# Seven block products for the hidden-dimension transform of 1024 rows, with kept sums of the sequence matrices

## The chip, the cores and the metric

The kernel runs on one core of a Trainium2 chip. The metric is device time in microseconds (us) of one execution, median of the runs. TensorE (PE) multiplies matrices, VectorE (DVE) and ScalarE (ACT) work elementwise, GpSimd (POOL) and SyncE (SP) here mostly issue transfers (DMAs) between the core's memory (SBUF) and the device memory.

## The reference

Four layers act on x of 2048 rows and 512 columns, each as x + f(layernorm(x)). Layers 0 and 2 mix (a Fourier transform as real matrix products), layers 1 and 3 are a gated feed-forward network.

```python
def mix(x, Cs, Ss, Cd, Sd):        # Cs, Ss: 2048x2048; Cd, Sd: 512x512
    a = x @ Cd.T                   # along the hidden dimension
    b = x @ Sd.T
    return Cs @ a - Ss @ b         # along the sequence
def ffn(x, w_gate, w_up, w_down):  # 512x1792, 512x1792, 1792x512
    return (gelu(x @ w_gate) * (x @ w_up)) @ w_down
x = x + mix(layernorm(x)); x = x + ffn(layernorm(x))
x = x + mix(layernorm(x)); x = x + ffn(layernorm(x))
```

Everything is float32. The kernel's matmuls read a rounded format (fp32r); each operand is split into a high and a low part and a product is made of three matmuls, hi·hi, hi·lo and lo·hi (`mm3`, lines 194 to 198). This triple is the unit of work.

## The kernel before

`mix` exchanges the order of the two transforms: it first multiplies the normalized rows z with the sequence matrices and then the result with the hidden matrices wh (cosine, and the sine with its sign turned by `split_minus`). The 2048 output rows are four blocks b of 512 (`NB`, `TB`). Per block the sequence products are done by seven block products instead of eight, in stages `a11`, `a12`, `s2` and `s4`; a `plan` gives the order. The block pieces A11, A12, A21, A22 of the sequence matrix are streamed from device memory in 128x512 tiles, and `make_s2` and `make_s4` form the sums S1 to S4 on VectorE (S1 = A21 + A22, S3 = A11 - A21, S2 = S1 - A11, S4 = A12 - S2). Layer 0 and layer 2 use the same matrices and form the same sums, each for itself. `plain` splits a tile into its two parts: the high one by ScalarE, the low one by VectorE (`split`, lines 145 to 149).

A block's sequence products leave eight tiles `cs[m, c]` (m: cosine or sine, c: which 128 of the 512 hidden columns), each 128 columns by 512 rows. `hid_groups` then multiplies them with wh: eight slices of wh, each with the four row tiles of the block, 32 triples, added up in four banks; `x_add` adds x, row tile by row tile, and stores the new x. So the two blocks that the change joins take 64 triples. In the plan the groups stand between the stages of a block (`EARLY_HID`, `MID_HID`, `LATE_HID`).

The next layer's norms are small pieces of work (`block_steps`): `norm` loads rows of x with `x_load_mixed`, normalizes and turns them by 32x32 transposes into a `wide` tile, which is stored, and `fetch` reads it back with the hidden dimension on the partitions. They are dealt out as `chores` in `hid_groups`, or queued and run one at each `step`.

Loads and stores: SyncE issues nearly all loads, in one order; `take`, `split_next` and `load_next` keep `AHEAD` + `RAW` items of the stream ahead of the product that uses them. GpSimd issues most stores and some loads, also in one order. SBUF is 94 slots of 128x512 (`NSLOT`) handed out in turn, oldest free one first, and two wide tiles that can be lent as four more slots each. A load into a slot waits until the slot's last reader is done. A scheduler sets the order of the instructions of each engine when the program is built.

The gated layers do the gate and up products, and some of the down products (`SEVEN`), as seven block products already. Their pieces are made once in layer 1 by `weight_steps` (load, four sums, splits, stores to device memory) and loaded again later. Down products made this way come out turned: `turned_rows` transposes them by 32x32 blocks into `xturned`, a wide tile with x, and `rows_done` stores it. In layer 3 with w = 1 the stored tile (`begun`) is read back by `begun_load`, and `plain_rows` adds the last products and writes `out`: these are the last instructions of the kernel.

Of the kernel before, what the change touches and what calls it, by code (L numbers as in the profile page):

```python
# [24 lines left out]
GELU_C = 0.044715  # L25
AHEAD = 7
# [9 lines left out]
SEVEN = {(1, 1): 5, (3, 0): 7, (3, 1): 5}  # L36
FORE = {0: 4, 2: 4}
# [6 lines left out]
def fnet_geglu(ctx: ExitStack, tc: tile.TileContext, x_in, ws, wh, wgu, wdn, wdc, out):  # L44
# [182 lines left out]
    def x_load_mixed(layer, i):  # L227

        g, n = divmod(i, NT)
        t = sb.get()  # L230
        for j in range(NT):
            r0 = j * P + n * 32
            nc.sync.dma_start(t[j * 32:(j + 1) * 32], xs[layer, g][r0:r0 + 32])
        return t

    def x_add(layer, i, t, ps, keep=False, engine=nc.gpsimd):

        plus(t, t, ps)
        ps8.put(ps)
        engine.dma_start(rows(layer + 1, i), t)  # L240
        if keep:
            fresh[i] = t
        else:
            sb.put(t)

# [19 lines left out]
    def down_piece(k, name):  # L265

        i = next(i for i, names in enumerate(pieces) if name in names)
        if i == 3:
            return wdd[k][:, 3 * 1024:]
        h = half[pieces[i].index(name)]  # L270
        return wdd[k][:, i * 1024:(i + 1) * 1024].rearrange("p (h c) -> p h c", h=2)[:, :, h]
# [55 lines left out]
    s1s, s2s, s3s, cs, held = {}, {}, {}, {}, {}  # L327
# [21 lines left out]
    def make_s2(k):  # L349
        def run(a21, a22, *a11):  # L350
            a11 = a11[0] if a11 else held.pop(k)
            plus(a22, a21, a22)
            minus(a21, a11, a21)
            minus(a11, a22, a11)
            s1s[k], s2s[k], s3s[k] = a22, a11, a21
            return split_slot(a11)
        return run
# [7 lines left out]
    def make_s4(k):  # L365
# [31 lines left out]

    def plan(layer):
# [31 lines left out]
    def mix_items(layer):  # L430
# [3 lines left out]
        for b, what in plan(layer):  # L434
# [9 lines left out]
            elif what == "S2":  # L444
                for i, k in skewed(3):
                    if i == 0:
                        raw(make_s2(k), a21[k], a22[k], *(() if hold else (a11[k],)))
                    else:
                        raw(make_s1(k) if i == 1 else make_s3(k))
            elif what == "S4":  # L450
                for i, k in skewed(2):
                    if i == 0:
                        raw(make_s4(k), a12[k])
                    else:
                        raw(plain, a22[k])
            else:
# [6 lines left out]
    for layer in range(0, 4, 2):  # L463
        mix_items(layer)
        for w in range(NB // 2):
# [7 lines left out]
            else:  # L473
                for near, products in zip(NEAR[1:], down_order(layer + 1, w)):
                    items.extend((F32R, (down_piece(k, name),), whole, near) for name, k in products)
# [126 lines left out]
    def block_steps(layer, w):  # L602
# [82 lines left out]
    def mix(layer):  # L685
        hid, sums, chores, hid_left = {}, {}, [], [0]

        def chores_at(b):
            if b == NB - 3:
# [127 lines left out]
        def s4(b):  # L817
            last = b == NB - 1
            if b == NB - 4:
                sb.reclaim("z")  # L820
            one, three = sides.pop(b)
# [16 lines left out]

        stages = {"A11": a11, "A12": a12, "S2": s2, "S4": s4}
        for n, (b, what) in enumerate(plan(layer)):  # L840
# [7 lines left out]
            if what in stages:  # L848
                stages[what](b)
            else:  # L850
# [55 lines left out]
    down_making = {}  # L906
# [27 lines left out]
    def geglu(w, layer):  # L934
# [71 lines left out]
        def up(n):  # L1006
            if layer == 1 and w == 1:
# [4 lines left out]
                if n % 2 == 0 and n // 2 + 1 in down_making:  # L1012
                    queue.extend(down_making.pop(n // 2 + 1)[1])
            if n + 3 in making:
# [97 lines left out]
        def ended(name, ps):  # L1112
# [3 lines left out]
            elif name == "A22":  # L1116
                for c in range(2):
                    turned_rows(0, 2 + c, ps[c])
                    ps8.put(ps[c])
                rows_done(0)  # L1120
            else:
# [6 lines left out]
                for c in range(2):  # L1128
                    turned_rows(name != "A12", 2 * (name in ("S1", "S3")) + c, to[c])
# [26 lines left out]
        def turned_view(at, part):  # L1156

            t = begun[part] if at == layer + 1 and pairs < NP else xs[at, w * 2 + part]
            return t.rearrange("(j t) (p e) -> p t j e", t=32, e=P)

        def rows_moved(at, part, run):

            for p in range(NT):
                v = xturned[part][p * 32:(p + 1) * 32]
                run(v.rearrange("t (j e) -> t j e", e=P), turned_view(at, part)[p])

        def load_turned(part):
            assert part or not sb.out("x")
            pool = tpool if part else upool
            xturned[part] = pool.tile([P, NT * D], F32, name="wide" if part else "xwide")  # L1170
            rows_moved(layer, part, lambda v, outside: nc.sync.dma_start(v, outside))

        def turned_rows(part, c, src):

            t = sb.get()
            blocks_of = "p (j e) -> p j e"
            nc.vector.transpose(t.rearrange(blocks_of, e=32), src.rearrange(blocks_of, e=32))
            to = xturned[part].rearrange("p (j c e) -> p j c e", c=NT, e=32)[:, :, c]
            plus(to, to, t.rearrange(blocks_of, e=32))
            sb.put(t)  # L1180

        def rows_done(part):
            rows_moved(layer + 1, part, lambda v, outside: nc.gpsimd.dma_start(outside, v))  # L1183
# [218 lines left out]
```

## Time and profile before

| what | value |
|---|---|
| three runs, median (lowest to highest) | 1620.7 us (1620.21 to 1622.89) |
| profiled execution | 1620.15 us |
| span of its trace | 1618.1 us |
| mean granted TensorE clock | 0.999 |
| matmuls on record | 7066 |
| bytes moved | 424.14 MB, 262 GB/s on average |

In the profile a busy share is an average over stages. A line such as `L197 PE MATMUL p<-s,s` is one line of the code, with output and inputs by the program's names without their numbers: `s` is a slot, `p` a bank, `wc` and `wb` pieces of weights in device memory, `x` the rows. Matmuls overlap: one lasts 389 ns on record while they start much closer together, so counts and starts say more than durations.

### The profile page before, as it was taken

What the parts mean: (1) busy time and instruction counts of PE and PEld (TensorE: products, weight loads), DVE (VectorE), ACT (ScalarE), POOL (GpSimd) and SP (SyncE); (2) the same over time, 40 slices, a digit from 0 to 9 for tenths busy, and PEclk for the clock granted to TensorE, in tenths of its full rate; (3) what the DMA queues carried; (4) which work ended last, traced back from release to release, by engine and by line L of the source; (5) the groups of instructions that cost most, each with busy time, mean ns of one, the idle gap of its engine ahead of it and who ended that gap; (6) DMA issues with size and microseconds to landing.
All of it is one profiled execution on the core that took longest, in us unless ns stands there. A gap on an engine that the chain in (4) does not pass through costs nothing.

```text
span 1618.1 us, 22784 instructions
## 1 busy us (share of the span) xinstructions
PE 1608.9 (99%) x7066; PEld 1326.0 (82%) x7066; DVE 1168.5 (72%) x2041; ACT 815.8 (50%) x1557; POOL 270.5 (17%) x477
## 2 busy tenths in 40 slices
PE   9999999999999999999999999999999999999998
PEld 6888888888888888888888888888888888888886
DVE  8996877889877655667887878787864557844573
ACT  7743453645766434556565434544445535433360
POOL 3111010152544113220120000010410000000002
PEclk9999999999999999999999999999999999999999
DMA  9767787899978799887887676868989776896455
GB/s 357 256 227 256 258 274 247 272 310 321 348 274 299 228 361 335 312 303 259 260 265 242 210 259 210 309 217 298 275 279 281 231 222 198 276 289 199 138 176 156
DMA packets 244937, 424.14 MB, mean 262 GB/s; under 512 B 28816, under 2 KB 82832, under 8 KB 243792
## 3 DMA queue, kind: packets, MB, share of 16 engines
q1 hardware_dynamic: 218016, 332.75, 64.1%
q0 software_dynamic: 26800, 89.94, 15.6%
q8 instruction: 56, 0.92, 0.2%
q14 instruction: 65, 0.53, 0.1%
HBM read 336.86 MB, written 85.72 MB: 261 GB/s over the span
## 4 chain that ended last, share of the span: by engine, by line
PE 96%; DMA 2%; DVE 1%; SPq 0%; issue 0%; ACT 0%; POOL 0%; DVEq 0%
PE p L196 32%; PE p L197 32%; PE p L198 32%; DMA s<-ws 1%; DMA out<-s 1%; PE p L749 0%; DMA s<-wb 0%; DVE s L149 0%; DMA s<-begun 0%; DVE s L180 0%; DMA xwide<-t 0%; DVE s L184 0%; DVE st L506 0%; SPq L224 0%; SPq L294 0%
## 5 line engine op out<-in xcount | busy, mean ns | idle before, releaser
L197 PE MATMUL p<-s,s 128*128 128x512 f32 x2334 | 906.6, 389 | 0.0
L198 PE MATMUL p<-s,s 128*128 128x512 f32 x2334 | 894.8, 389 | 0.3 <-DMA s<-wb 0.3
L196 PE MATMUL p<-s,s 128*128 128x512 f32 x2334 | 868.0, 390 | 0.5 <-ACT s L147 0.5
L147 ACT ACTIVATE s<-s 128x512 fp32r<-128x512 f32 (+1 forms) x764 | 437.9, 608 | 335.4 <-PE p L198 61.7
L149 DVE TENSOR_TENSOR s<-s,s 128x512 fp32r<-128x512 f32 (+1 forms) x764 | 483.8, 665 | 82.1 <-ACT s L147 67.0
L196 PEld LDWEIGHTS p<-s,s 128*128 128x128 f32 x2334 | 438.1, 188 | 93.1 <-ACT s L147 1.1
L197 PEld LDWEIGHTS p<-s,s 128*128 128x128 f32 x2334 | 438.2, 188 | 92.1 <-DVE s L149 0.7
L198 PEld LDWEIGHTS p<-s,s 128*128 128x128 f32 x2334 | 438.2, 188 | 92.1 <-DMA s<-wb 0.8
L184 DVE TENSOR_TENSOR s<-s,p 128x512 f32<-128x512 f32 x295 | 198.7, 683 | 232.3 <-PE p L198 127.3
L191 ACT ACTIVATE s<-p 128x512 f32<-128x512 f32 x217 | 127.2, 592 | 124.4 <-PE p L198 119.1
L180 DVE TENSOR_TENSOR s<-s,s 128x512 f32<-128x512 f32 (+1 forms) x305 | 184.7, 622 | 3.2 <-DMA s<-t 2.0
L931 ACT ACTIVATE s<-s 128x512 f32<-128x512 f32 x103 | 64.6, 629 | 83.0 <-DVE s L184 82.5
L147 ACT ACTIVATE s<-xwide 128x512 fp32r<-128x512 f32 (+1 forms) x90 | 53.3, 604 | 74.5 <-PE p L197 20.7
L519 POOL TENSOR_SCALAR rstd<-rstd 128x1 f32<-128x1 f32 x40 | 20.7, 517 | 350.0 <-ACT s L518 316.8
L149 DVE TENSOR_TENSOR s<-xwide,s 128x512 fp32r<-128x512 f32 (+1 forms) x90 | 58.5, 660 | 22.7 <-ACT s L147 22.3
L278 POOL DMA_DIRECT2D wb<-s x84 | 45.6, 545 | 58.3 <-ACT s L147 46.0
L516 ACT ACTIVATE s<-s 128x512 f32<-128x512 f32 x33 | 20.8, 630 | 68.0 <-PE p L198 27.6
L945 DVE TENSOR_TENSOR s<-s,s 128x512 f32<-128x512 f32 x75 | 51.8, 690 | 1.8
L240 POOL DMA_DIRECT2D x<-s x40 | 22.0, 550 | 162.2 <-DVE s L184 154.9
L538 ACT ACTIVATE s<-s,shift,rstd 128x512 f32<-128x512 f32 x53 | 42.5, 810 | 10.5 <-DVE shift L511 9.1
L187 DVE TENSOR_TENSOR s<-s,s 128x512 f32<-128x512 f32 (+1 forms) x69 | 40.9, 612 | 2.6 <-DMA s<-ws 2.6
L1183 POOL DMA_DIRECT2D begun<-xwide x8 | 5.2, 656 | 218.9 <-DVE xwide L187 218.9
(98 smaller groups left out, 581.9 us busy)
## 6 DMA issues: line engine op xcount, KB each, us to landing
s<-ws SPq DMA_DIRECT2D x381, 256.0 KB, 4.4
s<-wb SPq DMA_DIRECT2D x294, 256.0 KB, 4.9
s<-wc SPq DMA_DIRECT2D x119, 256.0 KB, 4.1
s<-wh SPq DMA_DIRECT2D x116, 256.0 KB, 5.3
wb<-s POOLq DMA_DIRECT2D x98, 256.0 KB, 4.5
s<-x SPq DMA_DIRECT2D x64, 256.0 KB, 5.1
xwide<-ws SPq DMA_DIRECT2D x51, 256.0 KB, 5.2
wc<-s POOLq DMA_DIRECT2D x49, 256.0 KB, 5.4
```

Source lines behind the costliest of these rows:

```text
L147: newest["ACT"] = nc.scalar.activation(hi, src, AF.Copy)
L149: newest["DVE"] = nc.vector.tensor_tensor(lo, src, f32(hi), op=ALU.subtract)
L180: nc.vector.tensor_tensor(out, a, b, op=ALU.subtract)
L184: bank_read["DVE"] = nc.vector.tensor_tensor(out, a, b, op=ALU.add)
L191: bank_read["ACT"] = nc.scalar.activation(v, src, AF.Copy)
L196: nc.tensor.matmul(ps, ah, bh, start=start, stop=False, skip_group_check=True)
L197: nc.tensor.matmul(ps, ah, bl, start=False, stop=False, skip_group_check=True)
L198: nc.tensor.matmul(ps, al, bh, start=False, stop=stop, skip_group_check=True)
L278: nc.gpsimd.dma_start(a, f32(t))
L538: nc.scalar.activation(z, x, AF.Identity, bias=shift, scale=rstd)
L931: nc.scalar.activation(t, g, AF.Gelu_apprx_tanh)
L945: nc.vector.tensor_tensor(t, t, v, op=ALU.mult)
```

## The change

In layer 2 blocks 0 and 1 are done together (`PAIRED`). Their hidden products become one stage `H` behind both blocks' sequence products: 1024 rows times wh as seven block products over four slices and two column halves. The pieces of wh (`whp`) are made in layer 1, w = 0, from a rearranged copy `whc`, by the same `weight_steps`. The results come out turned and are added to turned x. The norms of layer 3 that stood as chores in blocks 1 and 2 are queued behind `H`. The sums S1, S2 and S3 of blocks 0 to 2 are stored by GpSimd in layer 0 (`KEPT`) and loaded in layer 2 in place of A21, A22 and A11. Three things move besides: all `fetch` transfers go to GpSimd, the loads of `x_load_mixed` are ordered behind the stream's last load, and the last `begun` store goes to SyncE.

```diff
+HID_MADE = 3, 6, 8, 10
+HID_EARLY = 9
+KEPT = [("S1", "S2", "S3")] * 3 + [()]
+PAIRED = {0: 0, 2: 1}
...
@@ x_load_mixed
-            nc.sync.dma_start(t[j * 32:(j + 1) * 32], xs[layer, g][r0:r0 + 32])
+            with tc.issue_after(stream["last"].ins):
+                nc.sync.dma_start(t[j * 32:(j + 1) * 32], xs[layer, g][r0:r0 + 32])
...
+    def turned_moves(t, outside, run):
+        view = outside.rearrange("(j t) (p e) -> p t j e", t=32, e=P)
+        for p in range(NT):
+            run(t[p * 32:(p + 1) * 32].rearrange("t (j e) -> t j e", e=P), view[p])
...
+    def turned_add(x, c, src):
+        t = sb.get()
+        blocks_of = "p (j e) -> p j e"
+        nc.vector.transpose(t.rearrange(blocks_of, e=32), src.rearrange(blocks_of, e=32))
+        to = x.rearrange("p (j c e) -> p j c e", c=NT, e=32)[:, :, c]
+        plus(to, to, t.rearrange(blocks_of, e=32))
+        sb.put(t)
...
+    whp = {c: dram.tile([P, 7 * 512], F32, name=f"wp{c}") for c in range(ND)}
...
@@ make_s2, and new makers beside it
             s1s[k], s2s[k], s3s[k] = a22, a11, a21
+            for name, v in (("S1", a22), ("S3", a21)):
+                keep_sum(b, name, k, v)
...
+    def keep_sum(b, name, k, v):
+        if (b, name, k) in keep_s and (b, name, k) not in kept_s:
+            kept_s.add((b, name, k))
+            nc.gpsimd.dma_start(keep_s[b, name, k], v)
...
+    def make_s2_kept(k):
+        def run(v):
+            s2s[k] = v
+            return split_slot(v)
+        return run
...
@@ make_s4
             v = s2s.pop(k)
+            keep_sum(b, "S2", k, v)
             minus(a12, a12, v)
...
@@ plan
+            if paired(layer, b):
+                steps += [(b, "S2"), (b, "S4")] + ([(b, "H")] if b % 2 else [])
+                continue
...
+    HID_ORDER = [(name, c) for name in ("A11", "A12", "S2", "S3", "S1", "A22", "S4")
+                 for c in (range(ND) if name in ("A11", "A12") else (2, 3, 0, 1))]
...
@@ mix_items
+                    if layer and "S2" in KEPT[b]:
+                        raw(plain if i else make_s2_kept(k), keep_s[b, name, k])
...
+            elif what == "H":
+                items.extend((F32R, (piece(whp[c], name),), whole, AHEAD + RAW) for name, c in HID_ORDER)
...
@@ fetch
-                        (nc.gpsimd if w == 0 else nc.sync).dma_start(
+                        nc.gpsimd.dma_start(
...
@@ chores_at
+            if PAIRED[layer] and b < NB - 1:
+                return []
...
+        def hid_difference(name, c):
+            if name == "S2":
+                minus(hb["11", c], hb["12", c], hb["11", c])
+                hb["T2", c] = sb.get()
+                plus(hb["T2", c], hb["22", c], hb["11", c])
+            elif name == "S3":
+                plus(hb["12", c], hb["22", c], hb["12", c])
+            elif name == "A22":
+                minus(hb["21", c], hb["T2", c], hb["21", c])
+                sb.put(hb.pop(("T2", c)))
...
+        def hid_products(b):
+            for i, (name, c) in enumerate(HID_ORDER):
+                for more in HID_ORDER[i:i + HID_EARLY + 1]:
+                    hid_prepared(*more)
...
+                t, = take()
+                parts = hbs.pop((name, c))
+                first, last = i % ND == 0, i % ND == ND - 1
+                for j in range(2):
+                    hi, lo = (t[:, h][:, j * P:(j + 1) * P] for h in half)
+                    mm3(hbanks[at][j], (hi, lo), parts, name in ("A11", "A12", "S1") and first, last)
+                sb.put(t, *parts)
+                if last:
+                    hid_ended(name, hbanks[at])
+                step()
+            norms, others = block_steps(layer + 1, 0)
+            later.update(fetches=others[:ND], others=others[ND:])
+            queue.extend([None] * 12 + [run for norm in norms for run in (paced(norm), *[None] * 4)])
+
+        def hid_ended(name, ps):
+            if name in ("A11", "S2", "S3"):
+                hys[name] = [copied(p) for p in ps]
+                return
...
+            for j in range(2):
+                turned_add(hx[part], chunk + j, to[j])
...
+            if name in ("S4", "A22"):
+                to = xs[layer + 1, hid_block[0] - 1 + part]
+                turned_moves(hx.pop(part), to, lambda v, outside: nc.gpsimd.dma_start(outside, v))
...
@@ geglu, up
+            if layer == 1 and w == 0 and n in HID_MADE:
+                c = HID_MADE.index(n)
+                hid_making[c] = weight_steps(c, whc, whp)
+                hid_making[c][0]()
...
@@ rows_done
-            rows_moved(layer + 1, part, lambda v, outside: nc.gpsimd.dma_start(outside, v))
+            engine = nc.sync if part and layer == 3 and w else nc.gpsimd
+            to = begun[part] if pairs < NP else xs[layer + 1, w * 2 + part]
+            turned_moves(xturned[part], to, lambda v, outside: engine.dma_start(outside, v))
```

More of the change, by code (lines that the diff above doesn't have):

```diff
@@ L474, in fnet_geglu @@
                 for near, products in zip(NEAR[1:], down_order(layer + 1, w)):
[L475 removed]
+                    items.extend((F32R, (piece(wdd[k], name),), whole, near) for name, k in products)
                 items.extend((F32R, halves(wds[f]), whole, NEAR[2]) for f in range(2 * SEVEN[layer + 1, w], NF))
@@ L1154, in geglu @@
                 begun[part] = dram.tile([TB, D], F32, name=f"begun{layer}_{w}_{part}")
[L1156 to L1165, printed above, removed]
-        def load_turned(part):
[L1168 to L1180, printed above, removed]
+        def load_turned(part):
+            xturned[part] = wide_tile(part)
+            turned_moves(xturned[part], xs[layer, w * 2 + part], nc.sync.dma_start)
         def rows_done(part):
-            rows_moved(layer + 1, part, lambda v, outside: nc.gpsimd.dma_start(outside, v))
+            engine = nc.sync if part and layer == 3 and w else nc.gpsimd
+            to = begun[part] if pairs < NP else xs[layer + 1, w * 2 + part]
+            turned_moves(xturned[part], to, lambda v, outside: engine.dma_start(outside, v))
         xrows = []
```

98 lines of the change are left out of this document (85 added, 13 removed).

## The prediction

> **What bounds the kernel now.** I read the page first: busy times, the clock row, the chain that ended last. Then the table of stretches, to see in which of them TensorE ever stood still.
>
> ```profile
> span 1618.1 us, 22784 instructions
> ...
> PE 1608.9 (99%) x7066; PEld 1326.0 (82%) x7066; DVE 1168.5 (72%) x2041; ACT 815.8 (50%) x1557; POOL 270.5 (17%) x477
> ...
> PEclk9999999999999999999999999999999999999999
> ...
> PE 96%; DMA 2%; DVE 1%; SPq 0%; issue 0%; ACT 0%; POOL 0%; DVEq 0%
> ```
>
> TensorE is busy for 1608.9 of 1618.1 us at full clock and carries 96% of the chain that ended last. So the time is a count of matmuls times their pitch, plus 9.2 us in which TensorE waits. The stretches give the pitch and the place of the 9.2 us.
>
> ```profile
> core 0: us, PE busy (x) PEld busy (x) DVE busy (x) ACT busy (x) POOL busy (x), PEclk, DMA share, GB/s
> 385.00:800.00 415.00, 415.00 (x1832) 343.74 (x1832) 288.95 (x507) 237.59 (x481) 116.12 (x215) 1.00 0.87 301
> 800.00:1000.00 200.00, 200.00 (x885) 165.64 (x883) 164.90 (x313) 96.23 (x174) 23.67 (x36) 1.00 0.73 239
> 1000.00:1200.00 200.00, 200.00 (x884) 165.68 (x883) 154.53 (x253) 95.04 (x186) 30.29 (x58) 1.00 0.82 269
> 1600.00:1618.00 18.00, 11.72 (x52) 9.39 (x50) 3.31 (x5) 0.00 (x0) 2.19 (x4) 0.89 0.73 219
> ```
>
> 415.00 us for 1832 matmuls is 0.2265 us each. In the second mixing layer (inside 800 to 1200) TensorE never waits, so whatever lies beside it there is free, and every wait that the change brings there counts in full. The largest idle piece is the end: 18.00 less 11.72 is 6.3 us after the last matmul.
>
> **The matmuls.** Before, each of the two blocks takes 8 slices of wh times 4 row tiles, 32 triples; two blocks make 64. After, seven products over 4 slices and 2 column halves make 56. Eight triples less are 24 matmuls of the same shape, and the issue order of the changed program indeed has 24 rows fewer on TensorE. 24 times 0.2265 is **5.44 us off the path**, for nothing else fills TensorE there. Everything else in the change can only take from this, with one exception.
>
> **The end.** The change also sends the last `begun` store of the whole kernel (second half, layer 3, w = 1) from SyncE instead of GpSimd.
>
> The timelines of VectorE, GpSimd and TensorE (start, duration, operation) and the last step of the chain of waits:
>
> ```profile
> 1592.95 1.25 DVE L187 TENSOR_TENSOR wide<-wide,s 128x512 f32<-128x512 f32 x2
> ```
> ```profile
> 1594.44 2.20 POOL L1197 DMA_DIRECT2D s<-begun  x4 [5.35 <-DMA begun<-xwide]
> 1596.63 2.62 POOL L1183 DMA_DIRECT2D begun<-wide  x4
> 1607.93 2.30 POOL L1197 DMA_DIRECT2D s<-begun  x4 [8.68 <-DMA out<-s]
> ```
> ```profile
> 1611.33 0.39 PE L198 MATMUL p<-s,s 128*128 128x512 f32 x1
> ```
> ```profile
> 1614.06 0.69 DVE s L184
> ```
>
> VectorE has `wide` ready at 1594.20 (1592.95 plus 1.25). GpSimd issues its store only at 1596.63, because four loads of the other half wait ahead of it in its queue; the last four loads, which read that store back, leave at 1607.93. The releaser printed there is an `out` store; I read it as the landing of `begun<-wide`, whose data these loads need. The last addition starts at 1614.06, 2.3 us after the last matmul ended (1611.33 plus 0.39). From SyncE the store can go 2.4 us earlier, and its waiting loads with it. Then the last addition follows the matmul: from 0 (a slower landing eats it) to 2.3 us, and I take **2.2 us**, since the lead nearly equals the loss.
>
> **VectorE and ScalarE around the products.** The seven products need operands that the plain ones did not. In the second mixing layer 24 additions and 48 subtractions of kept sums go away, 16 sums for the products and 12 more splits come, and 8 transposes with 8 additions stand where 8 row additions from the banks stood. In total VectorE has four rows more in the whole order, so the load is not the question, but its place is: the sums that follow the last S4 bank stand together.
>
> VectorE's timeline where it never rests, and the page's group of ScalarE's bank copies:
>
> ```profile
> 902.40 1.28 DVE L180 TENSOR_TENSOR s<-s,s 128x512 f32<-128x512 f32 x2
> 903.60 0.68 DVE L149 TENSOR_TENSOR s<-s,s 128x512 fp32r<-128x512 f32 x1
> ```
> ```profile
> L191 ACT ACTIVATE s<-p 128x512 f32<-128x512 f32 x217 | 127.2, 592 | 124.4 <-PE p L198 119.1
> ```
>
> Two operations in 1.20 us: VectorE's pitch is 0.60 us back to back. In the issue order the low part of the first S2 operand is the 19th operation from the last S4 addition on: 19 times 0.60 is 11.4, with 0.4 for the bank 11.8 us. The matmul that reads it is the 52nd after S4, 52 times 0.2265 is 11.8 us. So VectorE is just in time: cost 0, up to 1.3 us if the pitch were the 0.68 of a single operation. Then S3 goes into the banks of S2 and must wait for ScalarE's copy: 0.39 for the last matmul plus 0.59 for the copy, against three pitches of 0.2265 to the waiting matmul, 0.68. I take **0.3 us**; it is 0 where the scheduler's filler matmuls come between, and not below.
>
> **Loads of the pieces of wh.** Slots are scarce while both blocks' results are held, so a piece's load is released late, and SyncE issues in order. Times to landing, from the view of the DMA queues (last column, median us):
>
> ```profile
> s<-wc SPq DMA_DIRECT2D x119, 256.0 KB, 4.1
> s<-wh SPq DMA_DIRECT2D x116, 256.0 KB, 5.3
> ...
> xwide<-x SPq DMA_DIRECT2D x24, 256.0 KB, 8.2
> ```
>
> Two of the 28 pieces have little lead. S1's first waits for the slot of a product that ends 30 matmuls after S4 and is needed at the 50th: 20 matmuls, 4.5 us. S1's second waits for VectorE's 33rd operation (33 times 0.60 and 0.4 is 20.2 us) and is needed at the 102nd matmul (23.1 us): 2.9 us. Landing takes 4.1 us for pieces of the same form (wc) and 5.3 for wh: short by 0 and 1.2, or by 0.8 and 2.4. Together 1.2 to 3.2, I take **2.0 us**. At the 8.2 us of the turned loads it would be 3.7 and 5.3, 9.0 us; this end stays for the range.
>
> **The rest of the second mixing layer.** The norms of the third layer's first two blocks leave the plain products of blocks 1 and 2 and queue up behind the seven products, with their loads of x. Those loads stand in SyncE's queue ahead of three kept sums, and wait for GpSimd to store the turned rows. From the last product to the need of the sum behind them are 105 matmuls, 23.8 us. The chain is bank 0.4, five operations of VectorE 3.0, four stores at 0.65 (the issue above) 2.6, a landing of 4.1 to 8.2, the load the same, its splits 1.3: 15.5 to 23.7 us. So it is covered, barely at the upper end: 0 to 2 us, and **0.5** taken.
>
> **DMA in layers 0 and 1.** The kept sums are 72 stores of 256 KB from GpSimd, 18.9 MB. The four wh slices are made into pieces beside the first gate and up products: four times 0.52 MB in and 1.84 MB out, 9.4 MB.
>
> Stretches again, in the columns shown above:
>
> ```profile
> 100.00:330.00 230.00, 230.00 (x1015) 190.19 (x1014) 186.70 (x310) 111.64 (x214) 32.73 (x53) 1.00 0.75 255
> 420.00:560.00 140.00, 140.00 (x619) 115.99 (x618) 99.87 (x181) 89.35 (x182) 57.65 (x107) 1.00 0.79 276
> ...
> 500.00:520.00 20.00, 20.00 (x90) 16.58 (x89) 13.94 (x27) 10.05 (x19) 8.92 (x17) 1.00 1.05 362
> 640.00:660.00 20.00, 20.00 (x90) 16.54 (x89) 12.61 (x23) 10.85 (x23) 3.97 (x8) 1.00 1.05 392
> ```
>
> TensorE has no idle time in the first two of these stretches, so nothing can be gained there. 18.9 MB over 230 us is 82 GB/s on top of 255: 337, below the 392 that one stretch sustained, with no wait. 9.4 MB over 140 us is 67 on top of 276; the busiest 20 us become 429, which is 37 GB/s over 392 and a backlog of 0.7 MB, 1.9 us of landing. ScalarE, VectorE and GpSimd have 50, 40 and 82 us of idle time there. Taken: **1.0 us**, between 0 and 3 in both layers together.
>
> The Trainium skill (DMA: Bandwidth & Descriptors, Specifications) puts HBM traffic of one core at about 358 GB/s. By that the same slice would run 71 GB/s over, an estimated backlog of 4.0 us, and this term would be nearer 3 than 1. The trace does not agree: 362 and 392 GB/s stand in it over 20 us each.
>
> **What moves queue.** The fetches of turned z for the second halves (32 DMAs of 64 KB in each of layers 1 and 3) go from SyncE to GpSimd. The stretch in which layer 3 does this, and the landing times by queue:
>
> ```profile
> 1380.00:1400.00 20.00, 19.66 (x86) 15.58 (x85) 16.49 (x28) 12.97 (x25) 0.00 (x0) 1.00 0.80 259
> ```
> ```profile
> s<-t SPq DMA_DIRECT2D x56, 64.0 KB, 2.7
> ...
> s<-t POOLq DMA_DIRECT2D x52, 64.0 KB, 5.8
> ```
>
> GpSimd does nothing in the stretch where layer 3 fetches, and TensorE loses 0.34 us there to loads on SyncE. So a gain of 0.3 is possible, and a loss of 3.1 (5.8 less 2.7) if the first half of the blocks were wanted at once; the products of the first half's end lie between. Taken: 0. The loads of turned x, eight of 256 KB, replace eight of the same size; they are issued a block early and delay nothing that the order shows. The ordering rule put on the mixed loads of x changes their place in the queue only.
>
> **The sum.** The profiled execution took 1620.15 us, 2.05 more than its span. 1620.15 less 5.44 and 2.2, plus 0.3, 2.0, 0.5 and 1.0, is 1616.3. The median of the runs is 0.55 above the profiled execution, which gives **1616.9 us**.
>
> **Rivals.** *Given back* (0.32): the same gains, but the waits sum to 5 to 9 us instead of 3.8: pieces at 5.3 us landing (3.2), copy 0.3, norms 2, DMA 2. That is 7.5 against 7.6 gained: 1620.6. For it speaks that the window of TensorE with no idle time at all allows no wait to hide; against it, that the stretches of the second mixing layer run at 239 and 269 GB/s, where landing should be short.
> *SyncE's queue takes the lead* (0.18): landing in the crowd of pieces, kept sums and turned rows is 8.2 us, as for `xwide<-x`. Then the two S1 pieces cost 9.0, the norms behind them 2, copy and layer 1 together 2: 13.0 against 7.6 gained, 1626.1. It decides from a landing of about 7 us on, where the two pieces cost 2.5 and 4.1, with copy, norms and DMA at 0.3, 2 and 2 10.9 in all, 3.3 more than is gained. Against: the turned loads of x are issued a block earlier, before S2 and S4, and should have landed by then.
> That the change does not do what it says has no chance worth a number: the matmuls are missing in the order.
> The forecast itself has 0.50, with its good end at waits of 1.2, 0.3, 0 and 0, 0.1 more at the end and 0.3 from the moved fetches: 1620.7 less 8.0 plus 1.5, 1614.2.
>
> **How the numbers follow.** A measurement of this kernel can tell about 0.2%, 3.2 us: faster means below 1617.5, slower above 1623.9. The forecast lies just past the line, so 0.50 for faster is the forecast's case with its better half and a little of its worse; given back is 0.32 for the same, the queue 0.18 for slower. The range goes from 1613.4, a little under the good end, to 1623.8, which leaves out most of the queue's case.
>
> **What would show it.** Right: TensorE has about 7042 records, pitch 0.2265; idle TensorE of 2 to 4 us between 1000 and 1100, released by loads of the wh pieces and ScalarE's copy; the last addition within 0.5 us of the last matmul. Wrong: idle TensorE in layers 0 or 1 of over 3 us (DMA); landing of `wp` loads over 7 us (the queue); no idle TensorE near 1030 to 1060 (then 1614); or the last addition still 2 us behind.

## The result and the profile after

| kernel | runs | median (lowest to highest) | profiled execution | span | granted clock |
|---|---|---|---|---|---|
| before | 6 | 1621.51 us (1620.21 to 1622.89) | 1620.15 us | 1618.1 us | 0.999 |
| changed | 6 | 1639.82 us (1637.81 to 1646.35) | 1638.77 us | 1637.0 us | 0.996 |

The change makes the kernel slower: ratio 1.0123, 95% interval 1.0111 to 1.0136. The forecast was 1616.9 us with a range to 1623.8, so it missed by 23 us and in sign. The page of the changed kernel, in the lines shown of before:

```profile
span 1637.0 us, 23162 instructions
...
PE 1612.3 (98%) x7042; PEld 1324.0 (81%) x7042; DVE 1168.5 (71%) x2043; ACT 837.3 (51%) x1591; POOL 351.3 (21%) x637
...
PE 90%; DMA 6%; DVE 1%; issue 1%; ACT 1%; POOL 1%; SPq 0%; DVEq 0%; POOLq 0%; ACTq 0%
```

The 24 matmuls are gone (7042 records for 7066), but TensorE is busy 3.4 us longer, and in the chain that ended last DMA has 6% instead of 2%. A full stretch of 20 us shows 90 matmuls (those that reach over an end count too), so every one missing stands for 0.2265 us. The stretches that lost most (after the busy times: PEclk, DMA share, GB/s):

```profile
520.00:540.00 20.00, 18.91 (x83) 15.03 (x83) 13.22 (x26) 11.08 (x21) 10.49 (x21) 1.00 1.01 336
580.00:600.00 20.00, 15.20 (x60) 11.74 (x59) 13.25 (x22) 7.28 (x13) 5.03 (x10) 0.91 0.89 270
1040.00:1060.00 20.00, 18.59 (x81) 14.75 (x80) 16.25 (x28) 10.14 (x19) 0.00 (x0) 1.00 0.83 270
1100.00:1120.00 20.00, 18.85 (x83) 15.28 (x82) 16.40 (x27) 10.53 (x23) 2.12 (x3) 1.00 1.13 254
1120.00:1140.00 20.00, 17.31 (x68) 13.51 (x68) 6.97 (x11) 8.87 (x20) 1.48 (x4) 0.91 0.89 293
1140.00:1160.00 20.00, 17.44 (x68) 13.40 (x67) 19.29 (x33) 12.70 (x28) 4.15 (x8) 0.91 1.00 366
1380.00:1400.00 20.00, 17.72 (x79) 14.32 (x78) 18.37 (x31) 8.84 (x15) 4.59 (x9) 1.00 1.07 312
```

They miss 7, 30, 9, 7, 22, 22 and 11 matmuls, 108 in all or 24.5 us. Four places: layer 1 where the pieces of wh are made (8.4 us), H itself (2.0), the stage behind H (11.6), and the end of the first half of layer 3 (2.5). The smaller gaps elsewhere, layer 0's above all, come to 2.0 us more, once what the kernel before misses itself is taken off (4 matmuls in the last of these stretches, for one). With 5.4 us gained by the matmuls and 2.6 at the end, 18.5 us are left, of 18.6 between the two profiled executions.

Idle time is not all of it. The granted clock in windows of 1 us, in the stage behind H:

```profile
1129.00:1130.00 1.00, 0.95 (x5) 0.45 (x3) 0.39 (x1) 0.97 (x3) 0.32 (x1) 1.00 0.92 328
1130.00:1131.00 1.00, 0.00 (x0) 0.00 (x0) 0.68 (x2) 0.60 (x1) 0.00 (x0) 1.00 0.91 297
1131.00:1132.00 1.00, 0.00 (x0) 0.00 (x0) 1.00 (x3) 0.05 (x1) 0.00 (x0) 1.00 1.01 369
1132.00:1133.00 1.00, 0.36 (x2) 0.30 (x2) 0.90 (x2) 1.00 (x2) 0.00 (x0) 1.00 1.14 314
1133.00:1134.00 1.00, 1.00 (x4) 0.56 (x3) 1.00 (x3) 0.18 (x1) 0.00 (x0) 0.82 0.99 211
1134.00:1135.00 1.00, 1.00 (x3) 0.73 (x3) 1.00 (x2) 0.46 (x1) 0.00 (x0) 0.50 1.05 287
1135.00:1136.00 1.00, 1.00 (x4) 0.78 (x3) 0.10 (x1) 0.77 (x2) 0.00 (x0) 0.50 1.00 340
1136.00:1137.00 1.00, 1.00 (x4) 0.81 (x3) 0.38 (x1) 0.00 (x0) 0.00 (x0) 0.50 1.02 363
1137.00:1138.00 1.00, 1.00 (x5) 0.81 (x5) 0.31 (x1) 0.59 (x1) 0.00 (x0) 0.98 0.79 279
```

TensorE stands still for 2.7 us (the longest wait for L154 in the view of waits below), then the clock is halved although it works without a pause; the rows from 1133 to 1138 us add up to 3.4 us at half. The chain of waits shows the pitch (second column) behind the stall at 590 us:

```profile
591.07 0.43 PE p L205
...
595.39 0.23 PE p L205
```

```profile
PE p L203 <- ACT s L154: 3.6, 2, 2.7
PE p L204 <- DMA s<-wd: 3.3, 1, 3.3
PE p L203 <- DMA s<-wc: 2.3, 1, 2.3
...
PE p L203 <- DMA s<-wp: 1.2, 1, 1.2
```

(Waits of TensorE in the changed kernel: us in total, times, longest.) In 3.4 us at 0.43 some 8 matmuls start where 15 would: 1.7 us more each time. The changed kernel has three such stretches (from 591, 1133 and 1150 us), some 5 of the 26 us. The third follows no long stall: between 1145.5 and 1150.4 us TensorE waits three times for 0.8 to 0.9 us, 2.6 in all. The Trainium skill (TensorE: Matmul & The Clock Gate, Part 1) says that the clock falls to half after an idle window of about 3.4 us and comes back after as long of steady work. The trace agrees on the half and on the way back (3.4 us); but 2.7 us of idleness were enough here, and at 1150 us 2.6 in three pieces.

What SyncE issues behind H, and what ScalarE then waits for (timelines; in brackets the idle time before and its releaser):

```profile
1095.76 0.42 SPq L259 DMA_DIRECT2D xwide<-x  x1
...
1096.76 1.66 SPq L259 DMA_DIRECT2D xwide<-x  x3
...
1107.00 2.57 SPq L259 DMA_DIRECT2D xwide<-x  x4
1109.86 4.04 SPq L323 DMA_DIRECT2D s<-wh  x4
1114.34 10.34 SPq L241 DMA_DIRECT2D s<-x  x12
```
```profile
1124.46 0.63 ACT L587 ACTIVATE s<-s 128x512 f32<-128x512 f32 x1 [7.40 <-DMA s<-x]
```

The first eight transfers are not H's: they are `load_turned` of layer 3, turned x in runs of 512 B, first read by VectorE at 1404.2 us. No line of the diff names them. The view of one tile's instructions places them in the two kernels (durations in ns; first and last start), before and changed:

```profile
L1171 SPq DMA_DIRECT2D xwide<-x x8: 315/325/1178, 1217.6 to 1240.6; - x8
```
```profile
L259 SPq DMA_DIRECT2D xwide<-x x8: 303/422/635, 1095.8 to 1109.1; - x8
```

In the kernel before, `xwide` is lent out as four slots through layer 2 and taken back at the start of layer 3. The change takes it back for H and does not lend it again, so the tile lies free after H, and the scheduler issues these loads 120 us early, into the stage behind H. In SyncE's own waits between 1095 and 1130 us the row loads of L241 wait four times, 3.4 us in all, for a landing of `xwide<-x`, and the loads of L323 three times, 2.2 us.

### The profile page after: what moved, and what is told of

The parts are those of the page before. It is cut to its first block, busy times and chain, and to the rows that moved or that the text cites. A ratio compares the mean times of both kernels' runs of the same rounds, so it can differ in the third digit from the quotient of the medians.

```text
span 1637.0 us, 23162 instructions
## 1 busy us (share of the span) xinstructions
PE 1612.3 (98%) x7042; PEld 1324.0 (81%) x7042; DVE 1168.5 (71%) x2043; ACT 837.3 (51%) x1591; POOL 351.3 (21%) x637
## 4 chain that ended last, share of the span: by engine, by line
PE 90%; DMA 6%; DVE 1%; issue 1%; ACT 1%; POOL 1%; SPq 0%; DVEq 0%; POOLq 0%; ACTq 0%
PE p L204 30%; PE p L205 30%; PE p L203 30%; DMA s<-ws 3%; DMA s<-x 1%; DVE s L156 1%; DMA wp<-s 1%; DMA s<-wd 1%; DMA s<-wh 1%; DMA s<-wc 0%; PE p L822 0%; DMA s<-wp 0%; DMA s<-m 0%; DVE s L191 0%; ACT s L154 0%
## 5 line engine op out<-in xcount | busy, mean ns | idle before, releaser
L154 ACT ACTIVATE s<-s 128x512 fp32r<-128x512 f32 (+1 forms) x816 | 467.4, 609 | 394.3 <-PE p L205 84.6
L156 DVE TENSOR_TENSOR s<-s,s 128x512 fp32r<-128x512 f32 (+1 forms) x816 | 516.9, 668 | 87.5 <-ACT s L154 71.6
L198 ACT ACTIVATE s<-p 128x512 f32<-128x512 f32 x224 | 131.3, 592 | 131.2 <-PE p L205 129.2
L187 DVE TENSOR_TENSOR s<-s,s 128x512 f32<-128x512 f32 (+1 forms) x304 | 181.9, 616 | 4.9 <-DMA s<-ws 3.7
L1103 ACT ACTIVATE s<-s 128x512 f32<-128x512 f32 x105 | 65.9, 629 | 93.3 <-DVE s L191 92.1
L705 POOL DMA_DIRECT2D s<-t x116 | 63.2, 550 | 74.5 <-PE p L205 42.4
L590 POOL TENSOR_SCALAR rstd<-rstd 128x1 f32<-128x1 f32 x40 | 14.3, 358 | 282.8 <-ACT s L589 248.4
L154 ACT ACTIVATE s<-xwide 128x512 fp32r<-128x512 f32 (+1 forms) x61 | 35.6, 594 | 37.6 <-DVE xwide L187 20.1
L396 POOL DMA_DIRECT2D S<-s x67 | 36.1, 540 | 71.3 <-DVE s L194 40.4
L194 DVE TENSOR_TENSOR s<-s,s 128x512 f32<-128x512 f32 (+1 forms) x62 | 36.4, 605 | 15.2 <-DMA s<-ws 12.6
L691 DVE STREAM_TRANSPOSE wide<-s 128x512 f32<-128x512 f32 x29 | 20.6, 709 | 36.8 <-ACT s L609 36.7
```

The costliest lines, as they stand in the source:

```text
L154: newest["ACT"] = nc.scalar.activation(hi, src, AF.Copy)
L156: newest["DVE"] = nc.vector.tensor_tensor(lo, src, f32(hi), op=ALU.subtract)
L187: nc.vector.tensor_tensor(out, a, b, op=ALU.subtract)
L198: bank_read["ACT"] = nc.scalar.activation(v, src, AF.Copy)
L705: nc.gpsimd.dma_start(to.rearrange("p (j t) -> p j t", t=P), cols.rearrange("(j p) t -> p j t", p=32))
L1103: nc.scalar.activation(t, g, AF.Gelu_apprx_tanh)
```

## The experiments

Each stands beside its own runs of the kernel before (median of these in the fourth column). The ratio is that of the means. "By the ratios" below means the difference of two ratios, times 1621 us; it serves for kernels that ran beside different runs of the kernel before.

| kernel | what it is | median us | before us | ratio, 95% interval |
|---|---|---|---|---|
| end_alone | before, last store on SyncE | 1618.90 | 1621.47 | 0.9984, 0.9975 to 0.9994 |
| sums_alone | changed, no H, no pieces | 1622.62 | 1621.47 | 1.0010, 0.9999 to 1.0021 |
| pieces_alone | changed, no H, no sums | 1633.52 | 1621.47 | 1.0076, 1.0061 to 1.0091 |
| rows_ahead | changed, fifth norm's rows earlier | 1641.05 | 1621.47 | 1.0123, 1.0103 to 1.0143 |
| x_lent | changed, xwide lent again | 1634.52 | 1622.52 | 1.0073, 1.0054 to 1.0093 |
| lent_fetch | x_lent, fetches as before | 1633.40 | 1622.52 | 1.0070, 1.0055 to 1.0085 |
| lent_fetch_early | lent_fetch, pieces earlier in layer 1 | 1631.70 | 1622.52 | 1.0061, 1.0045 to 1.0078 |
| lent_fetch_nosums | lent_fetch, no kept sums | 1643.81 | 1622.52 | 1.0137, 1.0120 to 1.0155 |
| moved | lent_fetch, pieces made in layer 2 | 1620.70 | 1621.46 | 0.9996, 0.9986 to 1.0005 |
| moved_once | moved, one turned load less | 1621.19 | 1621.46 | 0.9997, 0.9988 to 1.0007 |
| pieces_unstored | pieces_alone, pieces not stored | 1624.91 | 1621.46 | 1.0018, 1.0008 to 1.0027 |
| sums_fetch | sums_alone, fetches as before | 1620.46 | 1621.46 | 0.9995, 0.9986 to 1.0004 |
| moved_early5 | moved, HID_EARLY 5 | 1617.07 | 1620.67 | 0.9978, 0.9969 to 0.9987 |
| moved_early3 | moved, HID_EARLY 3 | 1639.30 | 1620.67 | 1.0109, 1.0092 to 1.0126 |
| early5_again | moved_early5 | 1617.81 | 1621.19 | 0.9979, 0.9969 to 0.9988 |
| end_again | end_alone | 1618.77 | 1621.19 | 0.9983, 0.9974 to 0.9992 |

### One part at a time

```diff
# end_alone (from before)
-            rows_moved(layer + 1, part, lambda v, outside: nc.gpsimd.dma_start(outside, v))
+            engine = nc.sync if part and layer == 3 and w else nc.gpsimd
+            rows_moved(layer + 1, part, lambda v, outside: engine.dma_start(outside, v))
# sums_alone and pieces_alone (from the changed kernel)
-PAIRED = {0: 0, 2: 1}
+PAIRED = {0: 0, 2: 0}
# sums_alone
-HID_MADE = 3, 6, 8, 10
+HID_MADE = ()
# pieces_alone
-KEPT = [("S1", "S2", "S3")] * 3 + [()]
+KEPT = [()] * 4
```

> The kernel before with one part of the change: the last begun store is issued by SyncE instead of GpSimd. Theory A (the trace after shows the last addition directly behind the last matmul): the 2.2 us between the end of the last matmul group and the last addition go, about 1619.3 against 1621.5 of the kernel before. Rival: the store's queue does not matter, since the loads of the same rows wait for its landing either way: within 1 us of the kernel before.

Measured: 2.6 us less. The end of its chain is the last matmul and then the last addition:

```profile
1612.80 0.24 PE p L198
1613.07 0.69 DVE s L184
```

> The changed kernel without the stage H and without the pieces of wh: the hidden products of layer 2 stand as before, while the kept sums, the fetches on GpSimd, the order of the row loads and the last store stay. Theory A (the time was lost in layer 1, where the pieces are made, and in layer 2, where H and the norms behind it stand): only layer 0's loss of about 1 us and the end's gain of 2.2 us are left, 1619 to 1622. Theory B (the 18.9 MB more that the kept sums store, or the moved fetches, hold the loads up everywhere): most of the loss stays, above 1630. If the moved fetches cause layer 1's stall: about 1628.

> The changed kernel without the kept sums and without the stage H, but with the pieces of wh made in layer 1 (nothing uses them). Theory A: layer 1 loses 8 to 9 us as in the changed kernel (in its trace 9 us of matmuls are missing between 520 and 600 us), less the end's 2.2 us: 1627 to 1629. Rival: the pieces are made beside other work and the loss there came with the kept sums' different state of slots and queues: 1618 to 1621.

The sums alone cost little more than expected, 1.1 us over before, which the interval does not tell from nothing. The pieces alone cost 12 us, more than expected. In the trace 9.3 us of matmuls are missing between 520 and 600 us, as in the changed kernel, but 6 more between 1360 and 1420 us, where nothing of the pieces stands. There the fetches run on GpSimd's queue; the timeline of GpSimd and the chain of pieces_alone:

```profile
1359.82 7.59 POOL L705 DMA_DIRECT2D s<-t  x14 [1.98 <-issue]
```
```profile
1374.02 8.16 DMA s<-wc
```

Fourteen small fetches leave in 7.6 us, and a down weight that SyncE issues behind them takes 8.2 us to land.

### The stage behind H

```diff
# rows_ahead: norm, layer 3, first half
+                if layer == 3 and not w:
+                    end = 2 * NT
-                for k in range(i if i == 0 or i + NT == end and not w else i + 2, min(i + 3, end)):
+                for k in range(i if i == 0 or i + NT == end and not w and layer == 1 else i + 2, min(i + 3, end)):
# x_lent: hid_products
+            lend("x")
             norms, others = block_steps(layer + 1, 0)
```

> The changed kernel with one thing other: the fifth norm behind H no longer loads its own three row tiles when it starts, they are loaded two norms ahead as for the other norms. Theory A (ScalarE stands in order behind the row loads from 1116.4 to 1124.5 us, the splits of the stage after H queue up behind it, TensorE starves and then runs at half its clock): the stalls between 1100 and 1160 us go, about 11 us less than the changed kernel, 1628 to 1630. Rival (H's own row loads and stores fill the DMA engines there, whose busy share is above 1.1, and TensorE starves on late loads whatever the norms do): 1636 to 1640.

> The changed kernel with one thing other: behind H the wide tile for turned x is lent out as four slots again, as it is all through layer 2 in the kernel before. In the changed kernel it lies free from the end of H on, and layer 3's loads of turned rows into it (eight of 256 KB in runs of 512 B, needed after 1225 us) are issued at 1095.8 to 1109.1 us, where in the kernel before they were issued at 1217.6 to 1240.6 us. Theory C (these early loads fill the DMA engines between 1100 and 1120 us, busy share 1.13 at 254 GB/s, and the rows of the norms and the tiles of the stage come late behind them): the 11.6 us of matmuls missing between 1100 and 1160 us fall to under 2, and the time to 1628 to 1631. Rival D (the stalls come from the norms being packed behind H and from H's own rows): 1636 to 1640, the stalls stay.

Theory A fell: with the rows loaded earlier nothing is won (1641.1), and 14.5 us are missing between 1100 and 1160 us instead of 11.6 (the profiled execution was the slowest of its four runs, 1645.5). The eight turned loads still stand there, at 1099.8 to 1137.7 us. Lending the tile out again puts them where they were, and the stretches of x_lent read:

```profile
L259 SPq DMA_DIRECT2D xwide<-x x8: 315/393/486, 1231.8 to 1246.6; - x8
```
```profile
1100.00:1120.00 20.00, 20.00 (x89) 16.17 (x88) 15.29 (x26) 12.58 (x30) 6.06 (x6) 1.00 0.85 266
1120.00:1140.00 20.00, 20.00 (x89) 16.32 (x87) 14.90 (x25) 9.19 (x16) 0.57 (x2) 1.00 0.99 368
1140.00:1160.00 20.00, 17.67 (x77) 14.27 (x77) 19.47 (x33) 13.89 (x31) 5.58 (x10) 1.00 0.83 293
```

The missing 11.6 us became 3.4, and the busy share of the DMA engines at 1100 us fell from 1.13 to 0.85. That is the way theory C said, but less far: under 2 us missing and 1628 to 1631 us were forecast. The time shows 5.3 us in the medians (1634.5 against 1639.8) and 8 by the ratios, where two runs of the changed kernel at 1646 us weigh in; layer 3 loses more in this kernel's trace (6.6 us between 1360 and 1420, against 3.6). The norms behind H, the prediction's suspect too, still stand there, so they account for at most the 3.4 us that are left. The one line took 8.2 us away; whether by the loads that go back or by the four slots that come free with it was not tried apart. SyncE's waits for these loads, above, speak for the loads.

### The fetches

```diff
# lent_fetch (from x_lent), sums_fetch (from sums_alone)
-                        nc.gpsimd.dma_start(
+                        (nc.gpsimd if w == 0 else nc.sync).dma_start(
```

> x_lent, and the fetches of a layer's second half go back to SyncE as before. Theory C: on GpSimd's queue they run ahead of everything (32 transfers of 64 KB in small runs between 1352 and 1378 us in the kernel with the pieces alone) and a weight piece lands 8.2 us after its issue; on SyncE they stand behind the loads that are due, so the 3 to 5 us lost at 1360 to 1420 us go: 2 to 4 us under x_lent, about 1627. Rival: only the place of the stall moves, within 1 us of x_lent.

> The kernel with the kept sums alone, and the fetches of a layer's second half on SyncE as before. Theory C: the 5.6 us of matmuls missing between 1360 and 1400 us come from the fetches on GpSimd's queue and fall to about 1; the rest stays: 1617 to 1619, under the kernel before by the end's 2.6 us less layer 0's 1 us. Rival: the kept sums themselves cost these us, 1621 to 1624.

In layer 3 the theory held: the stretch of sums_alone, and then of sums_fetch:

```profile
1360.00:1380.00 20.00, 17.44 (x70) 13.98 (x69) 16.54 (x28) 9.41 (x16) 5.29 (x10) 0.91 1.02 275
```
```profile
1360.00:1380.00 20.00, 19.66 (x87) 15.93 (x87) 16.16 (x28) 9.96 (x19) 0.00 (x0) 1.00 0.93 269
```

With the stretch behind it 5.7 us became 2.5, and the median fell by 2.2 us, less than expected: 1620.5 is over the 1617 to 1619 of theory C and under the rival's 1621. In lent_fetch layer 3's loss fell from 6.6 to 1.8 us, but between 520 and 600 us 13.8 are missing instead of 8.8: in layer 1 sixteen fetches now stand in SyncE's queue from 564 to 573 us, ahead of loads of `wd`. So the time is nearly unchanged (1.1 us in the medians, the intervals overlap), and the rival is right for this kernel.

### The pieces of wh

```diff
# lent_fetch_early (from lent_fetch)
-HID_MADE = 3, 6, 8, 10
+HID_MADE = 2, 4, 6, 8
# pieces_unstored (from pieces_alone): weight_steps, twice
+                    if place is not whp:
                         kept(to, t)
# moved (from lent_fetch): HID_MADE = (), and in mix, ahead of a stage
+            if layer == 2 and (b, what) == (0, "S2"):
+                for c in range(ND):
+                    load, rest = weight_steps(c, whc, whp)
+                    queue.extend([load, None, None, None, *rest])
```

> lent_fetch, with the four pieces of wh made at n = 2, 4, 6 and 8 of layer 1 instead of 3, 6, 8 and 10. Theory C (the last pieces hold twelve slots while the pieces of the down weights are due; the load due at 584 us was issued at 581.9, behind a slot that VectorE freed late): the 8 us lost at 520 to 600 us fall by half or more, 4 to 8 us under lent_fetch, 1619 to 1623. Rival (it is their traffic, 5.8 GB/s more in a stretch that is full anyway, wherever they are put): 1625 to 1629.

> The kernel with the pieces alone, whose pieces are loaded, summed and split in layer 1 as before but not stored (nothing uses them there), 7.3 MB less to move. Theory C (traffic): the 9.3 us missing between 520 and 600 us fall under 4, 1624 to 1628. Rival (fewer free slots and more work on ScalarE and VectorE): the loss stays, 1631 to 1634.

> lent_fetch, with the four pieces of wh made at the start of layer 2's S2 stage of block 0 (910 to 960 us, where the DMA engines' busy share of the changed kernel is 0.65 to 0.82) instead of in layer 1 (where it is 1.01 to 1.04 from 520 to 580 us). Theory C (the time was lost by transfers put where the DMA engines have no room): layer 1's loss of 8 to 14 us goes and nothing comes in its place, 1616 to 1620, at least 3 us under the kernel before run beside it. Rival (making the pieces costs TensorE wherever it is done, through VectorE, ScalarE and the slots): 1625 to 1632.

Made earlier, the loss moves with the pieces: 10.2 us are missing between 500 and 560 us, and 1631.7 us lies above what either side forecast. Not stored, the loss is gone: 1624.9 for 1633.5 us, and 0.5 us missing between 520 and 600 us, though the pieces are loaded, summed and split all the same. So it is the 7.3 MB of stores, and not the loads, sums and splits. (A slot also comes free some us sooner when its store is left out, so whether the stores cost through their traffic or through the slots they hold is open.) The stretches of before, then those of the changed kernel, show why there:

```profile
520.00:540.00 20.00, 20.00 (x90) 16.57 (x89) 13.46 (x24) 11.12 (x21) 8.09 (x15) 1.00 0.77 263
540.00:560.00 20.00, 20.00 (x90) 16.57 (x89) 13.13 (x22) 11.06 (x20) 0.00 (x0) 1.00 0.59 187
560.00:580.00 20.00, 20.00 (x90) 16.54 (x90) 14.52 (x24) 8.49 (x16) 0.00 (x0) 1.00 0.94 302
```
```profile
540.00:560.00 20.00, 20.00 (x90) 16.57 (x89) 16.03 (x29) 12.26 (x22) 12.53 (x24) 1.00 1.02 345
560.00:580.00 20.00, 20.00 (x90) 16.57 (x89) 11.72 (x19) 8.53 (x16) 12.51 (x23) 1.00 1.04 336
```

The pieces fill the pause that the DMA engines had just ahead of the down weights' loads. In the chain of the changed kernel one of these, which takes 8.7 us to land (median of `s<-wd` 5.3), is then too late, by the 3.3 us of the view of waits. In SyncE's queue a load of `wd` shortly ahead of it had also waited 3.1 us for a slot that VectorE freed.

```profile
581.85 8.67 DMA s<-wd
```

In layer 2, where they were put next, there is room. The busiest stretch of moved there:

```profile
920.00:940.00 20.00, 20.00 (x90) 16.56 (x89) 18.26 (x34) 11.14 (x20) 6.44 (x12) 1.00 1.01 374
```

No matmul is missing in it. moved takes 12 us off lent_fetch by the ratios, to 1620.7 us. Theory C (late transfers are all of it) asked for 1616 to 1620 us and 3 us under before, so something else was left.

### The kept sums, and one load less

```diff
# lent_fetch_nosums (from lent_fetch): KEPT = [()] * 4, and in s2, b == 0
-                lend("x")
+                if PAIRED[layer]:
+                    sb.reclaim("x")
+                else:
+                    lend("x")
# moved_once (from moved): beside
-                if k == pairs - 1:
+                if k == pairs - 1 and pairs < NP:
                     load_turned(0)
```

> lent_fetch without the kept sums: layer 2 forms S1, S2 and S3 itself as before, nothing is stored in layer 0. Here the wide tile for turned x is kept out of the slots from the first block of layer 2 on, so four slots fewer are free until H. Theory C: layer 0 gains 1 to 3 us and layer 2 pays nothing for 72 more operations of 0.6 us on VectorE: 1 to 3 us under lent_fetch. Rival (the sums are needed, since VectorE with the sums and H's differences is late): more than 5 us over lent_fetch.

> moved, without the first of the two loads of turned rows for layer 3, w = 0 (both kernels load this 1 MB tile twice and use the second load only). Theory C: 1 MB less in runs of 512 B at 1220 us, where nothing is late: no change, within 1 us of moved. Rival: the loads there hold up the start of layer 3, 1 to 2 us less.

Without the kept sums the kernel is 10 us slower, as the rival said. Layer 0 gains the 3 us that theory C hoped for, but 12.2 us are missing in H (1040 to 1100 us) instead of 2.3, and 5.2 more at 940 to 960. The stretch of H in that kernel:

```profile
1060.00:1080.00 20.00, 16.84 (x63) 11.78 (x61) 20.00 (x34) 6.63 (x11) 0.00 (x0) 0.90 0.79 246
```

VectorE is busy for all of it, and TensorE waits for it and for ScalarE. It looks as if the kept sums make room on VectorE for H's operands; how much of the 10 us is due to the four slots that this kernel lacks is not told apart. The one load less changes nothing, as expected.

### VectorE at the start of H

```diff
# moved_early5, moved_early3 (from moved)
-HID_EARLY = 9
+HID_EARLY = 5 or 3
```

> moved, where H prepares its operands five products ahead instead of nine, so that VectorE, which works without a pause from 1015.3 to 1034.1 us in moved, does the operands of the first products before differences that are needed later. If VectorE's crowding at H's start is what is left there: the 2.0 us missing between 1020 and 1040 us go, 1 to 2 us under moved. If it is the load of the piece of wh (1.1 us of waiting in moved): no change, within 1 us.

> The same with three products ahead. If VectorE's crowding is the cause, as good as five or, where an operand is now too late, up to 3 us worse than moved, with TensorE waiting for VectorE inside H; if it is the load: no change.

The stretch of H's start, in moved, moved_early5 and moved_early3:

```profile
1020.00:1040.00 20.00, 18.66 (x81) 14.81 (x81) 17.61 (x30) 10.27 (x19) 0.00 (x0) 1.00 0.66 192
```
```profile
1020.00:1040.00 20.00, 19.31 (x86) 15.67 (x85) 17.64 (x29) 12.80 (x24) 0.00 (x0) 1.00 0.70 212
```
```profile
1020.00:1040.00 20.00, 15.02 (x52) 11.22 (x52) 14.50 (x24) 7.04 (x13) 0.00 (x0) 0.83 0.49 144
```

Five takes 2.9 us off moved by the ratios, where 1 to 2 were expected. In this stretch 1.1 of the 2.0 missing us are won. The 1.1 us of waiting for a piece of wh is gone as well (TensorE waits 0.7 us for ScalarE's copy instead), so the lead of nine had made that load late too. How is not shown: between 1031 and 1037 us in moved, SyncE waits 3.5 us for slots that matmuls free and 1.4 us for one that VectorE frees, and operands made early hold slots themselves. At 1100 to 1120 us 1.6 us are won too, but moved_once, with nine, misses nothing there either, so this is not shown to come from the five. Three is too late: 8.6 us lost here, 11.1 at 1100 us, TensorE waiting for VectorE and ScalarE and then at half clock; 18 us over moved by the ratios, where at most 3 were expected.

### Against the last store alone

> moved_early5 once more, beside end_alone on the same chip. If the 24 matmuls fewer pay something once the late transfers are repaired: 1 to 3 us under end_alone. If only the last store pays: the same as end_alone within 1 us.

> The kernel before with only the last store moved, once more beside moved_early5: about 2.5 us under the kernel before, 1618 to 1619.

The repaired kernel (moved_early5) is faster than the kernel before (0.9979), and so is end_alone (0.9983). Their difference, 1.0 us in the medians, is on the expected side, but the intervals overlap: whether the seven products pay anything beyond the last store is not settled. The two traces say where the gain stays: of the stretches with a gap, early5_again misses 12 matmuls in layer 0, 7 at H and behind it and 18 between 1360 and 1400 us, end_again 5, none and 6. These 26 more are 5.9 us, about what 24 matmuls fewer save.

## Why the prediction was wrong, step by step

- **The matmuls**: right. 24 records fewer at the same pitch wherever TensorE does not wait.
- **The end**: right. 2.2 us forecast, 2.6 measured by end_alone (ratio 0.9984); in the changed kernel the chain ends without a gap:

```profile
1632.95 0.24 PE p L205
1633.21 0.69 DVE s L191
```

- **VectorE and ScalarE around the products**: the copy was right (0.2 us for 0.3). VectorE "just in time" for the first operand was near (its bound at a pitch of 0.68 is 1.5 us, not 1.3), but the lead of nine products cost about 1 us of the 2.0 missing in H, through VectorE's order or through slots (moved_early5).
- **Loads of the pieces**: 2.0 forecast, 2.0 us missing between 1040 and 1060 us, with 1.2 us of waiting for `wp`. Just ahead of that load SyncE waits 3.3 us for matmuls, the kind of cause that the prediction named (the slot of a product). The landing was shorter than feared (the last column is the median to landing), so *SyncE's queue takes the lead* fell with its mechanism, though the time came out on its side.

```profile
s<-wp SPq DMA_DIRECT2D x28, 256.0 KB, 3.4
```

- **The rest of the second mixing layer**: 0.5 forecast, 11.6 lost. The failed step is the sentence, under *What moves queue*, that the turned loads "delay nothing that the order shows". It counted H's eight and left out layer 3's eight, which the change moves by 120 us to 1095.8 to 1109.1 us. With the tile lent again, 8.2 of the 11.6 us are gone. It is a moved step with nothing in the diff to name it.
- **DMA in layers 0 and 1**: 1.0 forecast, at most 3. The kept sums kept to it (sums_fetch is 1.6 us over end_alone). The pieces cost 8 to 9 us, the sign of being wrong that the prediction had named itself (over 3 us in layers 0 or 1). The failed step is the average over 420 to 560 us: it spread 9.4 MB over 140 us and looked at the busiest 20 us inside, while most of the damage came behind, at 580 to 600 us, when a pause ahead of the down weights' loads had been filled. The Trainium skill's limit of about 358 GB/s (DMA: Bandwidth & Descriptors, Specifications), half of what two cores share, would have warned in the right direction. For this one core the runs show no such limit: 374 GB/s over 20 us without a missing matmul, above.
- **What moves queue**: 0 forecast, 2 to 5 us measured. "GpSimd does nothing in the stretch" was the fault: the idle queue issued the fetches early and together (fourteen in 7.6 us, above). The 0.34 us that the prediction read as lost before in layer 3 is TensorE's idle time; 4 matmuls are missing there, 0.9 us.
- **The clock**: missing from every term. Each wait was priced at its length; the three stretches at half clock cost 1.7 us each on top.
- *Given back* named what happened in kind, waits that eat the gain, but with 7.5 us of them where some 26 came.

## What to carry to other kernels

After a change to how buffers are lent or freed, compare the whole issue order of each DMA queue, not only the changed lines: a buffer that lies free draws in any load that waits for it. Where TensorE is nearly always busy, a pause of the DMA engines may be what lets the next loads land in time; look at what stands in the 20 to 40 us behind the new traffic. Here the same pieces cost 8 us and more ahead of the down weights' loads and nothing at 920 us. Price a stall of several us, or several short ones together, with the half clock that can follow (1.7 us here).

## What the runs showed of the hardware

- The granted clock falls to 0.50 for 3.4 us after a stall, but these runs give no one length for it. It fell after 2.7 us without a matmul and after three waits of 0.8 to 0.9 us close together (changed kernel, 1133 and 1150 us), and after a single wait of 2.0 us in rows_ahead (1109.7 us). It stayed at 1.00 after 2.3 us (the wait for `wc` in the changed kernel, in the stretch from 1380 us).
- Loads in runs of 512 B take the DMA engines longer than their bytes tell: between 1100 and 1120 us they moved 254 GB/s at a busy share of 1.13, at 540 to 560 us 345 GB/s at 1.02. In x_lent the slow stretch goes where these loads go: 233 GB/s at 1.12 from 1240 to 1250 us. Other transfers run beside them in both.
